# Attention output kept in weight slots and stored once per pair, with reordered start, gating and end, in a fused attention and mixture-of-experts kernel

## Chip, cores and metric

The kernel runs on one core of a Trainium2 chip. The metric is the device time of one execution in microseconds (us), lower is better. All inputs and outputs lie in HBM.

## What is computed

The reference runs three layers one after the other: attention over 4 batches, 8 heads, 576 positions and 64 dimensions, then a mixture of experts in which each token goes to one expert of at most 288 tokens, then a second mixture of experts with 32 slots.

```
attn = softmax(q_d k_d) v_d, repeated 4 times along the positions   # q_d, k_d, v_d: means over 4 positions
     + softmax over |i - j| < 4 of (q k) times v
x    = attn as 2304 rows of 512
logits = x @ w_gate                     # 8 experts
assigned = greedy by falling logit, at most 288 tokens to an expert
y[mask_e] = relu(x[mask_e] @ w1[e]) @ w2[e]
logits2 = y @ phi                       # 32 slots
d = softmax of logits2 over the tokens;  c = softmax over the slots
slot_out[e] = relu((d.T @ y)[e] @ m2w1[e]) @ m2w2[e]
out = c @ slot_out
```

## The kernel before, in words

Everything is written by hand: each stage is a function, and lists of stage names fix the order in which every engine gets its instructions. An engine runs its own instructions in that order and waits where one needs something. There are four parts.

**Attention** (`attention`, lines 37 to 376). The work is cut into 8 units; a unit is two heads by two batches, and 4 units make a pair of batches. One unit loads `k` (two transfers, 576 KB together), `q` (576 KB), `v` (1008 KB) and `vp` (two transfers, 640 KB), 2800 KB in all; SyncE (SP) issues these loads. GpSimd makes the sums over 4 positions (`pool_k`, `pool_q`, `pool_v`). TensorE makes the banded scores (`l_scores`, lines 120 to 133, which opens with the mask matmul of L126 and goes on with 72 matmuls of L131), the coarse scores (`d_scores`), transposes (`l_tr`, `d_tr`) and products with the values (`d_av`, `l_av`, line 282). VectorE takes maxima, sums and divisions (`l_max`, `d_max`, `l_norm`, `d_norm`) and adds both results to `xT` (`l_add`); ScalarE does the exponentials (`l_exp`, `d_exp`) and copies out of PSUM (`l_tr`, L216; `d_tr_out`; `d_out`). `l_x` (lines 305 to 313) transposes `xT` back in three groups of three tiles and ScalarE copies each group into the tile `xu`, of which there are two buffers: unit u writes the buffer of unit u - 2. `l_st` (lines 322 to 325) stores `xu` of a unit to `x_dram` in HBM; ScalarE issues this transfer, 576 KB in runs of 512 bytes. `l_logit` and `l_lg` make the gate logits.

The order is `FIRST` (unit 0 and the start of unit 1), then `UNIT0` once, then `UNIT` for units 1 to 8, where the second entry is relative to the period's unit. A period of `UNIT` holds `l_scores` of the next unit early and `d_tr` of the next unit late, `l_x(0, 0)` of its own unit, `l_x(-1, 1)`, `l_x(-1, 2)` and `l_st(-1)` of the unit before, the loads of the unit two ahead, and at its end `pump`, which loads one weight half (1 MB, `w2t`) into a free slot in periods 2 to 6 and fills all free slots in period 7.

**Weight slots** (`Stream`, lines 862 to 919). All expert weights are streamed in halves of 1 MB through named slots of SBUF: `a0` to `a8`, `b0` to `b7`, and tiles of the attention that have become free (`V2`, `kT1`, `V0`). `pump` pairs the next weight on the list with the next free slot and has SP issue the load; `release` gives a slot back. SP takes its transfers in program order, so one that waits holds back those behind it.

**Gating** (`gating`, lines 583 to 858). Five rounds move thresholds until each expert has at most 288 tokens; a round is a chain through VectorE, ScalarE and TensorE. TensorE fills its free time with `PMaker.product` (lines 517 to 528): 16 products `P` of `phi` and the `w2t` halves, of 32 matmuls each (L525), taken off PSUM by `turn` (L537, VectorE). Before: two products after the first transposes, two in each of the five rounds, one after the sums of `dispatch`, three at the end of `dispatch`; two `turn` in each round, two in `dispatch` ahead of L756, one ahead of L776, three at the end. `dispatch` (lines 739 to 791) computes the rows of each expert (`totals`: L698, L699), writes `idx`, and calls `first_gather`, three indirect transfers that fetch expert 0's rows of `x_dram`. Then a branch (L851) on all engines asks whether more rounds are needed.

**Experts and end** (`moe`, lines 1151 to 1487). `START`, `PERIOD`, `END` and `LAST` order the stages of the 8 experts: `x_t` (transposes of the gathered rows), `split` (weights into two parts: ScalarE L1196, VectorE L1198), `hidden` (TensorE, L1211 to L1214), and so on down to `weighted` (L1309) and `slots` (L1331). In `weighted` four PSUM tiles `m`, `l`, `g`, `t` are written (`m`, `l`, `h`, `t` for the last expert). `l` is also what `soft_lt` (L1274) reads. `FINISH` orders the second layer's own work: `c_load` loads the logits `lg`, `c_soft` is their softmax on VectorE, `first` (L1427), `first_t` (L1438), `second` (L1449), `gathered`, `combine` (L1479).

Of the kernel before, what the change touches and what calls it, by code (L numbers as in the profile page):

```python
# [36 lines left out]
def attention(nc, tc, ctx, kv, q, k, v, vp, C, x_dram, logit_tok, wg, pump):  # L37
# [296 lines left out]
    stages = dict(load_k=load_k, load_q=load_q, load_v=load_v, load_p=load_p, pool_k=pool_k, pool_q=pool_q, pool_v=pool_v,  # L334
# [23 lines left out]
    load_p(0)  # L358
    load_v(0)
# [44 lines left out]
UNIT0 = [
    ("l_tr", 0, 0),
    ("l_tr", 0, 1),
    ("load_v", 2),
    ("pool_q", 1),
    ("d_av", 0),
    ("load_p", 2),  # L410
    ("d_out", 0),
    ("l_max", 1),
    ("d_scores", 1),
    ("d_max", 1),
    ("pool_v", 1),
    ("l_exp", 1),
    ("l_norm", 1),
    ("d_exp", 1),
    ("l_tr", 0, 2),
    ("d_norm", 1),  # L420
    ("l_av", 0),
    ("pump", 0),
    ("d_tr", 1),
    ("l_add", 0),
    ("pool_q", 2),
    ("l_x", 0, 0),
]
UNIT = [
    ("d_tr_out", 0),
    ("load_k", 2),  # L430
    ("pool_k", 1, 0),
    ("pool_k", 1, 1),
    ("load_q", 2),
    ("l_scores", 1),
# [18 lines left out]
    ("load_p", 2),
    ("l_x", 0, 0),
    ("l_x", -1, 2),
    ("l_norm", 1),
    ("l_lg", -1),
# [53 lines left out]
class PMaker:  # L511
# [71 lines left out]
def gating(nc, tc, ctx, L, C, Z, idx, fill, first, force=None):  # L583
# [10 lines left out]
    def psum(shape):  # L594
        return ps.tile(shape, F32, name="t", bufs=4)
# [15 lines left out]
    fill.products(psum)  # L611
# [44 lines left out]
    def rounds(n, start=False):  # L656
        for r in range(n):
# [12 lines left out]
            fill.turn()  # L670
            fill.turn()
# [16 lines left out]
            fill.products(psum)  # L688
# [233 lines left out]
def halves(kind, es):  # L922
# [15 lines left out]
    ("first_t", 0, 1),  # L938
# [703 lines left out]
```

## Time and profile before

| what | us |
|---|---|
| median of 3 runs (424.38 to 428.44) | 428.37 |
| the profiled execution | 427.75 |
| its span, first to last instruction | 426.0 |
| mean granted TensorE clock of the span, share of full | 0.917 |
| TensorE busy | 360.7 (85%) |
| VectorE, ScalarE, GpSimd busy | 235.9, 180.5, 127.4 |

All times in the rows further down count from the span's start. The profiled execution lies 0.62 us under the median and has 1.75 us around its span. Attention reaches to 150.4, gating to 195.9, the experts to 375, the end to 426. A busy share is an average over stages with different limits, so each stage has to be read by itself: the timeline names in square brackets how long an engine was idle before an instruction and what ended that.

### The profile page before, as it was taken

The numbers are of one execution on the slowest core, as the hardware profiler recorded it, in microseconds if no ns is written. First come the engines' busy times: TensorE is split into PE (matmuls) and PEld (weight loads), VectorE is DVE, ScalarE is ACT, GpSimd is POOL, SyncE is SP. The second block draws the span as 40 slices with busy tenths as digits, with TensorE's granted clock in tenths as the row PEclk, the third lists the DMA queues.
The fourth block names the chain that finished last, engine by engine and source line by source line (L and its number), as shares of the span: only waits on it lengthen the run. The fifth ranks groups of instructions, "written<-read, shape, count | busy, mean of one in ns | idle before, by whom it ended". The sixth has DMA issues, their size and how long they took to land. (4 is left out here: it accounts for less than half of the span.)

```text
span 426.0 us, 12313 instructions
## 1 busy us (share of the span) xinstructions
PE 360.7 (85%) x5116; PEld 270.1 (63%) x5116; DVE 235.9 (55%) x636; ACT 180.5 (42%) x497; POOL 127.4 (30%) x167
## 2 busy tenths in 40 slices
PE   0779989899559876757899999999999898689994
PEld 0456666666328556656878787887879685233693
DVE  4653647645505189763456676665758475424253
ACT  6362765567135434103545454453636343101231
POOL 6466663725340000042205050505141102240000
PEclk9885999989855899966999999999999999989997
DMA  8999978798997798934485999999997696989965
GB/s 230 274 268 246 205 201 274 226 291 264 260 397 275 226 382 310 425 109 161 157 295 195 329 333 335 353 360 323 363 321 254 230 390 267 373 320 411 408 244 217
DMA packets 31962, 122.52 MB, mean 288 GB/s; under 512 B 3232, under 2 KB 13088, under 8 KB 22688
## 3 DMA queue, kind: packets, MB, share of 16 engines
q1 hardware_dynamic: 19968, 111.85, 76.7%
q10 hardware_dynamic: 9632, 4.85, 4.1%
q0 software_dynamic: 2304, 5.02, 4.0%
q8 instruction: 41, 0.67, 0.7%
q14 instruction: 17, 0.14, 0.1%
HBM read 111.97 MB, written 9.73 MB: 286 GB/s over the span
## 5 line engine op out<-in xcount | busy, mean ns | idle before, releaser
L1293 POOL DMA_INDIRECT lg_rows<-lt,idx x24 | 24.6, 1026 | 114.0 <-DVE lt L1274 109.1
L1211 PE MATMUL h<-V,wh 128*128 128x288 f32 x128 | 37.9, 317 | 2.3 <-ACT V L1188 1.1
L1211 PE MATMUL t<-V,wh 128*128 128x288 f32 x128 | 37.9, 318 | 1.6 <-ACT wh L1196 1.6
L1212 PE MATMUL h<-V,wh 128*128 128x288 f32 x128 | 36.5, 306 | 0.5 <-DVE a L887 0.5
L1212 PE MATMUL t<-V,wh 128*128 128x288 f32 x128 | 35.0, 296 | 0.0
L216 ACT ACTIVATE aT<-t 38x384 f32<-38x384 f32 (+1 forms) x48 | 21.5, 448 | 26.4 <-PE t L212 25.6
L1198 DVE TENSOR_TENSOR wl<-b,wh 128x512 fp32r<-128x512 f32 x32 | 21.7, 682 | 18.7 <-ACT wh L1196 18.5
L1211 PEld LDWEIGHTS t<-V,wh 128*128 128x128 f32 x128 | 24.1, 188 | 8.5 <-issue 5.7
L1226 DVE STREAM_TRANSPOSE V<-hT 128x288 f32<-128x288 f32 x64 | 27.1, 453 | 4.1 <-issue 4.1
L1211 PEld LDWEIGHTS h<-V,wh 128*128 128x128 f32 x128 | 25.1, 196 | 6.4 <-issue 2.8
L1198 DVE TENSOR_TENSOR wl<-a,wh 128x512 fp32r<-128x512 f32 x32 | 21.7, 678 | 11.2 <-ACT wh L1196 10.7
L180 DVE TENSOR_REDUCE lg<-D 128x6 f32<-128x864 f32 x8 | 8.5, 1067 | 34.6 <-PE D L172 34.6
L1196 ACT ACTIVATE wh<-b 128x512 fp32r<-128x512 f32 x32 | 20.0, 631 | 16.4 <-DVEq L851 10.5
L1175 POOL DMA_INDIRECT kT<-x_dram,idx x21 | 20.2, 963 | 21.0 <-PE t L1186 17.0
L1212 PEld LDWEIGHTS h<-V,wh 128*128 128x128 f32 x128 | 25.2, 197 | 0.8 <-DVE a L887 0.8
L1220 ACT ACTIVATE hT<-h 128x288 f32<-128x288 f32 x32 | 13.1, 409 | 29.7 <-PE m L1243 15.3
L1212 PEld LDWEIGHTS t<-V,wh 128*128 128x128 f32 x128 | 24.1, 189 | 0.1
L1196 ACT ACTIVATE wh<-a 128x512 fp32r<-128x512 f32 x32 | 20.3, 633 | 8.5 <-PE h L1212 5.0
L282 PE MATMUL S<-aT,V 102*64 102x64 f32 x512 | 19.4, 239 | 5.0 <-ACT aT L216 2.9
L1214 PE MATMUL h<-V,wl 128*128 128x288 f32 x128 | 22.8, 301 | 0.0
L313 ACT ACTIVATE xu<-t 128x384 f32<-128x384 f32 x24 | 10.8, 485 | 27.9 <-DMA x_dram<-xu 17.4
L282 PEld LDWEIGHTS S<-aT,V 102*64 102x64 f32 x512 | 17.9, 152 | 7.3 <-ACT aT L216 3.1
(310 smaller groups left out, 963.5 us busy)
## 6 DMA issues: line engine op xcount, KB each, us to landing
a<-in_moe_w_dram SPq DMA_DIRECT2D x27, 1024.0 KB, 7.8
b<-in_moe_w_dram SPq DMA_DIRECT2D x21, 1024.0 KB, 12.1
a<-in_moe_w2t_dram SPq DMA_DIRECT2D x9, 1024.0 KB, 8.7
V<-in_v_dram SPq DMA_DIRECT2D x8, 1008.0 KB, 12.8
kT<-in_k_dram SPq DMA_DIRECT2D x16, 288.0 KB, 11.5
qT<-in_q_dram SPq DMA_DIRECT2D x8, 576.0 KB, 12.8
x_dram<-xu ACTq DMA_DIRECT2D x8, 576.0 KB, 13.7
vp<-in_vp_dram SPq DMA_DIRECT2D x8, 512.0 KB, 13.6
```

The source lines that it names most:

```text
L216: nc.scalar.activation(aT[sl, 3 * g:3 * g + n, :, r], p[sl, 0:n].rearrange("p s (c q) -> p s c q", c=4), AF.Copy)
L282: nc.tensor.matmul(p[64 * h:64 * h + 64, k // 2, o:o + 64], rows_v(s, slice(0, 64 + W), 2 * k + h, c), aT[0:64 + W, 2 * k + h, c].rearrang ...
L313: nc.scalar.activation(s["xu"][:, 3 * g:3 * g + 3], p, AF.Copy)
L1175: nc.gpsimd.indirect_dma_start(out=xs[0:96, DM * c:DM * c + DM], out_offset=None, in_=x_dram, in_offset=bass.IndirectOffsetOnAxis(ap=idx[: ...
L1196: nc.scalar.activation(wh, w, AF.Copy)
L1198: nc.vector.tensor_sub(wl, w, wh.bitcast(F32))
L1211: nc.tensor.matmul(p, wh[:, dt], xh[:, dt], start=dt == 0, stop=False)
L1212: nc.tensor.matmul(p, wh[:, dt], xl[:, dt], start=False, stop=False)
L1214: nc.tensor.matmul(p, wl[:, dt], xh[:, dt], start=False, stop=dt == 3)
L1220: nc.scalar.activation(h, st.pop(("ph", e, ft)), AF.Relu)
L1226: nc.vector.transpose(st["hb", e][:, :, ft], st.pop(("hr", e, ft)).rearrange("p (b t) -> p b t", t=32))
L1293: nc.gpsimd.indirect_dma_start(out=lg_rows[3 * e + c], out_offset=bass.IndirectOffsetOnAxis(ap=idx[:, 3 * e + c:3 * e + c + 1], axis=0), i ...
```

## The change

Six parts. (1) `xu` is gone: the four units of a pair write their 128 columns of `x` into shared tiles of full rows, two weight slots (`a5`, `a6` for the first pair, `a7`, `a8` for the second) and a small tile `xu8`. `l_x` takes groups of 4, 4 and 1 tiles. (2) `l_st` only does something for the last unit of a pair: SP, no longer ScalarE, issues three transfers with runs of 8 KB (2 KB for the third), 2.36 MB together. The weight stream has `a0` to `a4` during attention, gets `a5`, `a6` in period 7 and `a7`, `a8` behind `b7`. In `UNIT` the `pump` comes ahead of `load_p` and `l_st` behind it. (3) `FIRST`, `UNIT0` and `UNIT` are reordered; `warm` issues matmuls whose result nobody reads, 10, 16 and 10 in `FIRST`. (4) Gating: three products at first, two in four rounds, one in the fifth, four after `totals`; rounds take all made products off, `dispatch` only at its end; five PSUM buffers in place of four. (5) `warm` in the experts' first period (8, then 2 after each of two `x_t`) and in `LAST` (2, 3, 2, 3); `weighted` of the last expert uses `m`, `h`, `h`, `t`. (6) `FINISH`: `first_t` follows its `first` closer, and `second(3, 1)` and `gathered(3, ...)` come ahead of `combine(2, ...)`.

```
     def l_x(u, g):
-        s = st[u]
-        xT = s["xT"].rearrange("d b s -> d (b s)").rearrange("d (t i) -> d t i", i=128)
-        p = tpsum([128, 3, 128])
-        for i in range(3):
-            nc.tensor.transpose(p[:, i], xT[:, 3 * g + i], ident)
-        if g == 0:
-            s["xu"] = sb.tile([128, 9, 128], F32, name="xu")
-        nc.scalar.activation(s["xu"][:, 3 * g:3 * g + 3], p, AF.Copy)
+        pr, hp = divmod(u, 4)
+        xT = st[u]["xT"].rearrange("d b s -> d (b s)").rearrange("d (t i) -> d t i", i=128)
+        n = (4, 4, 1)[g]
+        p = tpsum([128, n, 128])
+        for i in range(n):
+            nc.tensor.transpose(p[:, i], xT[:, 4 * g + i], ident)
+        if hp == 0:
+            if g < 2:
+                x = wa.tile([128, 2048], F32, name=f"a{5 + 2 * pr + g}").rearrange("p (t d) -> p t d", d=DM)
+            else:
+                x = sb.tile([128, 1, DM], F32, name="xu8")
+            st["xu", pr, g] = x
+        nc.scalar.activation(st["xu", pr, g][:, :, 128 * hp:128 * hp + 128], p, AF.Copy)
...
     def l_st(u):
         pr, hp = divmod(u, 4)
-        nc.scalar.dma_start(x_dram.rearrange("(p j) d -> p j d", j=NT)[:, 9 * pr:9 * pr + 9, 128 * hp:128 * hp + 128],
-                          st.pop(u)["xu"])
+        st.pop(u)
+        if hp == 3:
+            rows = x_dram.rearrange("(p j) d -> p j d", j=NT)
+            for g in range(3):
+                n = (4, 4, 1)[g]
+                nc.sync.dma_start(rows[:, 9 * pr + 4 * g:9 * pr + 4 * g + n], st.pop(("xu", pr, g)))
...
+    def warm(u, n):
+
+        w = ident.bitcast(BF16)
+        p = tpsum([128, 256])
+        for _ in range(n):
+            nc.tensor.matmul(p, w[:, 0:128], w[:, 0:256], start=True, stop=True)
...
-    fill.products(psum)
+    for _ in range(3):
+        fill.product(psum)
...
-            fill.turn()
-            fill.turn()
+            while fill.made:
+                fill.turn()
...
-            fill.products(psum)
+            for _ in range(1 if start and r == n - 1 else 2):
+                fill.product(psum)
...
         zs, inc = totals()
+        if what is not None:
+            for _ in range(4):
+                fill.product(psum)
...
-        if what is not None:
-            fill.turn()
-            fill.turn()
-            fill.product(psum)
-
...
             u = above()
-            fill.turn()
...
-            for _ in range(3):
-                fill.product(psum)
-            for _ in range(3):
+            while fill.made:
                 fill.turn()
...
-        names = "m", "l", "g" if e < E - 1 else "h", "t"
+        names = ("m", "l", "g", "t") if e < E - 1 else ("m", "h", "h", "t")
...
+    def warm(e, n):
+
+        w = ident.bitcast(BF16)
+        p = ps.tile([128, 2, 256], F32, name="t", bufs=3)
+        for _ in range(n):
+            nc.tensor.matmul(p, w[:, 0:128], w[:, None, :].to_broadcast([128, 2, 256]), start=True, stop=True)
...
-    WS.free = [(wa, f"a{i}") for i in range(9)]
+    WS.free = [(wa, f"a{i}") for i in range(5)]
...
-                WS.free += [(kv, x) for x in ("V2", "kT1", "V0")]
+                WS.free += [(wa, "a5"), (wa, "a6")] + [(kv, x) for x in ("V2", "kT1", "V0")]
...
         WS.add_slots(wb, [f"b{i}" for i in range(8)])
+        WS.add_slots(wa, ["a7", "a8"])
```

The new order of the first unit, and what moves in the other lists:

```
FIRST: load_k 1, load_p 0, pool_k 0, l_scores 0, pool_q 0, load_q 1, load_v 0, d_scores 0, warm 10, l_max 0,
       l_exp 0, warm 16, d_max 0, load_p 1, l_norm 0, d_exp 0, load_v 1, load_k 2, pool_k (1, 0), warm 10,
       d_norm 0, l_scores 1, d_tr 0, d_tr_out 0, pool_k (1, 1), pool_v 0, load_q 2, load_v 2, l_tr (0, 0)
UNIT0: d_av 0, d_out 0, l_max 1, load_p 2, l_tr (0, 1), pool_q 1, d_scores 1, d_max 1, l_tr (0, 2), l_exp 1,
       pool_v 1, l_norm 1, d_exp 1, pump, pool_q 2, l_av 0, d_norm 1, d_tr 1, l_add 0, l_x (0, 0)
UNIT, engine by engine: l_logit(-1) behind l_tr(0, 1); d_out(0) ahead of l_tr(0, 2); pump ahead of load_p(2);
       l_st(-1) last but d_tr(1)
LAST:  warm 2 behind soft_exp, 3 behind weighted_out, 2 behind weighted_t, 3 behind slots_acc
FINISH: first 0 0, selection, c_soft, first 0 1, first_t 0 0, first 1 0, first_t 0 1, c_parts 0, first 1 1, ...
       second 3 0, second 3 1, combine 2 1, gathered 3 0, gathered 3 1, combine 2 0, combine 3 0, combine 3 1
```

## Rows read from the trace of the kernel before

**Rows 1.** Windows: stretch, its us, busy per engine, granted clock, DMA share, GB/s

```profile
100.00:120.00 20.00, 11.75 (x222) 8.51 (x218) 8.79 (x19) 7.30 (x26) 8.81 (x9) 0.83 1.04 300
...
0.00:60.00 60.00, 42.24 (x689) 29.32 (x689) 30.67 (x69) 31.93 (x89) 37.12 (x55) 0.86 1.00 246
...
67.23:80.38 13.15, 12.35 (x240) 8.68 (x235) 8.93 (x21) 7.76 (x27) 5.25 (x7) 1.00 0.97 293
...
110.00:138.50 28.50, 19.46 (x239) 13.80 (x234) 9.03 (x19) 9.82 (x31) 9.39 (x13) 0.58 0.91 314
...
138.50:150.40 11.90, 10.73 (x138) 6.96 (x136) 2.39 (x6) 5.98 (x15) 0.00 (x0) 0.86 0.75 249
...
195.90:202.00 6.10, 5.62 (x22) 5.30 (x23) 1.73 (x5) 0.93 (x2) 1.84 (x2) 0.50 0.78 269
202.00:340.00 138.00, 135.74 (x1572) 111.19 (x1571) 87.75 (x232) 67.16 (x164) 36.16 (x36) 1.00 0.86 296
...
376.20:379.50 3.30, 3.30 (x20) 0.87 (x16) 0.00 (x0) 0.00 (x0) 2.70 (x11) 0.50 1.00 415
```

The columns after the us are busy us (and instructions) of PE, PEld, DVE, ACT and POOL; a DMA share of 1.00 is all 16 engines busy.

**Rows 2.** Waits of ACT and of SP: us in total, times, longest us

```profile
ACT xu L313 <- DMA x_dram<-xu: 17.4, 3, 11.8
...
SPq L891 <- DMA x_dram<-xu: 66.4, 6, 14.4
...
SPq L88 <- DMA x_dram<-xu: 11.6, 1, 11.6
```

**Rows 3.** DMA issues between 97 and 103: size, us from issue to landing

```profile
x_dram<-xu ACTq DMA_DIRECT2D x1, 576.0 KB, 22.1
```

**Rows 4.** Timeline of ACT and PE, units 5 to 7: start, us, engine, line

```profile
97.30 0.42 ACTq L324 DMA_DIRECT2D x_dram<-xu  x1
...
110.00 0.47 PE L126 MATMUL S<-mask,identb 128*128 128x380 bf16 x2
...
112.76 2.09 PE L131 MATMUL S<-kT,qT 128*32 128x76 f32 x72 [2.30 <-DMA qT<-in_q_dram]
...
119.47 0.87 ACT L313 ACTIVATE xu<-t 128x384 f32<-128x384 f32 x2 [11.77 <-DMA x_dram<-xu]
```

**Rows 5.** Timeline of PE, end of the first unit

```profile
32.62 1.12 PE L282 MATMUL S<-aT,V 102*64 102x64 f32 x16 [2.92 <-ACT aT L216]
...
38.16 0.78 PE L126 MATMUL S<-mask,identb 128*128 128x380 bf16 x2
```

**Rows 6.** Timeline from the last round of gating to the first expert

```profile
177.90 0.38 DVE L644 TENSOR_TENSOR Z<-key,best 128x72 bf16<-128x72 f32 x2
178.93 0.42 PE L698 MATMUL g<-Z,onesb 128*128 128x144 bf16 x1
...
180.88 0.50 DVE L537 STREAM_TRANSPOSE P<-t 128x128 f32<-128x128 f32 x2
...
189.39 0.92 POOL L1146 DMA_INDIRECT kT<-x_dram,idx  x1 [0.30 <-remote]
...
192.23 0.32 DVE L537 STREAM_TRANSPOSE P<-t 128x128 f32<-128x128 f32 x1 [1.18 <-PE t L525]
...
195.92 0.61 PE L1211 MATMUL h<-V,wh 128*128 128x288 f32 x1 [1.14 <-ACT V L1188]
```

**Rows 7.** DMA issues between 186 and 194: us from issue to landing

```profile
kT<-x_dram,idx POOLq DMA_INDIRECT x3, 3.5
```

**Rows 8.** Timeline of PE and DVE, last expert and end

```profile
366.62 0.37 PE L1309 MATMUL l<-V,dT 32*32 32x256 f32 x1 [0.94 <-DVE lt L1274]
...
381.57 0.75 DVE L1394 TENSOR_REDUCE cmx<-lg 128x18 f32<-128x576 f32 x1 [6.32 <-DMA lg<-lg_rows]
...
385.83 0.69 DVE L1169 TENSOR_SCALAR h<-h 128x512 f32<-128x512 f32 x1
...
388.57 0.62 PE L1427 MATMUL h<-kT,sT 128*32 128x512 f32 x1 [0.74 <-ACT h L1167]
...
418.43 0.63 PE L1479 MATMUL h<-R,V 128*128 128x128 f32 x4 [1.09 <-DVE R L1467]
```

More of the change, by code (lines that the diff above doesn't have):

```diff
@@ L34, in dap, with attention @@
     return bass.AP(tensor=t.tensor, offset=t.offset + offset, ap=[list(d) for d in dims])
-def attention(nc, tc, ctx, kv, q, k, v, vp, C, x_dram, logit_tok, wg, pump):
+def attention(nc, tc, ctx, kv, wa, q, k, v, vp, C, x_dram, logit_tok, wg, pump):
     ident = C["ident"]
@@ L380 @@
     ("load_k", 1),
+    ("load_p", 0),
     ("pool_k", 0, 0),
+    ("pool_k", 0, 1),
+    ("l_scores", 0),
+    ("pool_q", 0),
     ("load_q", 1),
-    ("pool_k", 0, 1),
-    ("pool_q", 0),
+    ("load_v", 0),
     ("d_scores", 0),
+    ("warm", 0, 10),
+    ("l_max", 0),
+    ("l_exp", 0),
+    ("warm", 0, 16),
     ("d_max", 0),
     ("load_p", 1),
+    ("l_norm", 0),
     ("d_exp", 0),
-    ("l_scores", 0),
     ("load_v", 1),
-    ("l_max", 0),
+    ("load_k", 2),
+    ("pool_k", 1, 0),
+    ("warm", 0, 10),
     ("d_norm", 0),
-    ("pool_k", 1, 0),
-    ("l_exp", 0),
+    ("l_scores", 1),
     ("d_tr", 0),
     ("d_tr_out", 0),
-    ("load_k", 2),
+    ("pool_k", 1, 1),
     ("pool_v", 0),
-    ("pool_k", 1, 1),
-    ("l_norm", 0),
     ("load_q", 2),
-    ("l_scores", 1),
+    ("load_v", 2),
+    ("l_tr", 0, 0),
 ]
 UNIT0 = [
[L405 to L408, printed above, removed]
     ("d_av", 0),
-    ("load_p", 2),
     ("d_out", 0),
     ("l_max", 1),
+    ("load_p", 2),
+    ("l_tr", 0, 1),
+    ("pool_q", 1),
     ("d_scores", 1),
     ("d_max", 1),
+    ("l_tr", 0, 2),
+    ("l_exp", 1),
     ("pool_v", 1),
-    ("l_exp", 1),
     ("l_norm", 1),
     ("d_exp", 1),
-    ("l_tr", 0, 2),
+    ("pump", 0),
+    ("pool_q", 2),
+    ("l_av", 0),
     ("d_norm", 1),
-    ("l_av", 0),
-    ("pump", 0),
     ("d_tr", 1),
     ("l_add", 0),
-    ("pool_q", 2),
     ("l_x", 0, 0),
@@ L437 @@
     ("l_max", 1),
-    ("load_v", 2),
+    ("load_q", 2),
+    ("l_tr", 0, 1),
     ("l_logit", -1),
-    ("l_tr", 0, 1),
     ("l_exp", 1),
     ("d_scores", 1),
+    ("d_max", 1),
+    ("d_out", 0),
     ("l_tr", 0, 2),
-    ("d_out", 0),
-    ("d_max", 1),
+    ("pool_v", 1),
+    ("l_av", 0),
     ("d_exp", 1),
-    ("l_av", 0),
+    ("load_v", 2),
+    ("l_x", -1, 1),
     ("l_add", 0),
-    ("l_x", -1, 1),
     ("d_norm", 1),
-    ("pool_v", 1),
-    ("pool_q", 2),
[L453 to L457, printed above, removed]
+    ("l_norm", 1),
+    ("l_x", 0, 0),
+    ("l_lg", -1),
+    ("l_x", -1, 2),
+    ("pump", 0),
+    ("load_p", 2),
+    ("pool_q", 2),
     ("l_st", -1),
     ("d_tr", 1),
-    ("pump", 0),
 ]
@@ L594, in psum @@
     def psum(shape):
-        return ps.tile(shape, F32, name="t", bufs=4)
+        return ps.tile(shape, F32, name="t", bufs=5)
     mm = one.tile([128, 2], F32, name="mm")
@@ L932 @@
     ("first", 0, 1),
+    ("first_t", 0, 0),
     ("first", 1, 0),
-    ("first_t", 0, 0),
+    ("first_t", 0, 1),
     ("c_parts", 0),
@@ L959 @@
     ("second", 3, 0),
+    ("second", 3, 1),
     ("combine", 2, 1),
-    ("second", 3, 1),
-    ("combine", 2, 0),
     ("gathered", 3, 0),
     ("gathered", 3, 1),
+    ("combine", 2, 0),
     ("combine", 3, 0),
@@ L1129 @@
     ("soft_exp", -1),
+    ("warm", -1, 2),
     ("soft_d", -1),
@@ L1135 @@
     ("weighted_out", -1),
+    ("warm", -1, 3),
     ("weighted_sum", -1),
     ("weighted_t", -1),
+    ("warm", -1, 2),
     ("slots", -1),
     ("slots_acc", -1),
+    ("warm", -1, 3),
 ]
@@ L1341, in slots_acc @@
             nc.vector.scalar_tensor_tensor(acc, acc, cor[e % 2], p, op0=ALU.mult, op1=ALU.add)
-    def psum(shape):
-        return ps.tile(shape, F32, name="t", bufs=3)
-    stages = dict(hidden=hidden, relu=relu, split=split, x_t=x_t, gather=gather, h_rows=h_rows,
+    def warm(e, n):
[3 more added lines that the diff above has]
+            nc.tensor.matmul(p, w[:, 0:128], w[:, None, :].to_broadcast([128, 2, 256]), start=True, stop=True)
+    stages = dict(warm=warm, hidden=hidden, relu=relu, split=split, x_t=x_t, gather=gather, h_rows=h_rows,
                   logits2=logits2, logits2_out=logits2_out, soft=soft, soft_exp=soft_exp, soft_d=soft_d, soft_lt=soft_lt, scatter=scatter, weighted=weighted, weighted_out=weighted_out, weighted_sum=weighted_sum,
@@ L1360, in moe @@
             split(0, 2)
+            warm(e, 8)
         for name, rel, *args in START if e <= 0 else PERIOD if e < E - 1 else END if e < E else LAST:
@@ L1363, in moe @@
                 stages[name](e + rel, *args)
+                if e == -1 and name == "x_t" and args[0] < 2:
+                    warm(e, 2)
                 if (name, e + rel) == ("weighted_out", E - 1):
@@ L1543, in pump @@
                 WS.once += ["V2", "V0"]
-                WS.free += [(kv, x) for x in ("V2", "kT1", "V0")]
+                WS.free += [(wa, "a5"), (wa, "a6")] + [(kv, x) for x in ("V2", "kT1", "V0")]
             WS.pump((0, 0, 1, 1, 1, 1, 1, None)[u])
-        attention(nc, tc, actx, kv, q, k, v, vp, C, x_dram, L, wg, pump)
+        attention(nc, tc, actx, kv, wa, q, k, v, vp, C, x_dram, L, wg, pump)
     wb = ctx.enter_context(tc.tile_pool(name="wb", bufs=1, reuse_waits="tile"))
```

15 lines of the change are left out of this document (4 added, 11 removed).

## Prediction

> **What bounds the kernel now.** I read the windows first, then the waits, the DMA issues of the place where they are long, and the timelines around it. The windows [rows 1] show two kinds of stretch. From 202 to 340 TensorE is busy 135.74 of 138 us at the full clock: it is the bound there, the change touches nothing in it, and it can only be shifted as a block. Before 150.4 it is otherwise: an undisturbed attention period (67.23 to 80.38) takes 13.15 us with 12.35 of PE, but the last full one (110 to 138.5) takes 28.50 with 19.46 of PE at a granted clock of 0.58. Something starves it, and the clock falls with it.
>
> The waits say what [rows 2]: ScalarE's copy into `xu` waits 17.4 us in three pieces, the longest 11.8, for the store of `x`, and SP's loads wait 66.4 and 11.6 us for the same stores, since they get their completion behind them. The DMA view gives the cause [rows 3]: a 576 KB store takes 22.1 us to land. The timeline puts it together [rows 4]: the store issued at 97.30 lands near 119.4, and the copy at 119.47 has stood 11.77 us for it. With it stands all that ScalarE issues behind (exponentials, copies of transposes), and so PE. Before that, the scores of unit 7 opened at 110.00, but their matmuls waited 2.30 us for `q` and came at 112.76: DMA was at a share of 1.04 [rows 1]. So two bounds lie close together up to 110: PE's period and the load stream. Which of them is late once the stall goes is the main question.
>
> **Attention, part by part.** The profiled execution took 427.75 us, 0.62 under the median; I sum against it and add 0.62 at the end.
>
> (a) First unit. `l_av` (L282) waits 2.92 us for ScalarE's copies, which stand behind `l_exp(1)` [rows 5]; the new order has `l_tr(0, 1)` ahead of them and `l_tr(0, 2)` ahead of `l_exp(1)`. That gives 2.9, and a further 1 us from the clock, which is 0.86 over 0 to 60 [rows 1]: unit 2's mask matmul comes at 34 in place of 38.16 (-4). The 36 `warm` matmuls lie in gaps of PE (42.24 busy of 60 [rows 1]). No row has this form; by the 0.78 us of a pair of L126 [rows 5] (380 columns, against 256) one takes 0.13 to 0.26, all 36 between 4.7 and 9.5 us. If the cover is gone, (a) is worth +1 to +5; if the clock comes up at once, -7.
>
> (b) The stall. No store comes before the last unit of a pair, and no tile is written twice in a pair, so the 17.4 us of ScalarE's waits go, and SP's waits on stores too. From 38.16 to 110.00 are five periods of 14.4 us; at 13.15 each, PE would open unit 7 at 34 + 65.8 = 99.8.
>
> (c) What is late next: `q` of unit 7. Ahead of its landing lie seven units (7 x 2.867 MB), `k` and `q` (1.18), three weight halves (3.15) and the first pair's store (2.36): 26.8 MB. Two rows bound the rate. At 246 GB/s all along (0 to 60, share 1.00) it lands at 108.8; with 60 us at 246 (14.8 MB) and the other 12.0 MB at 300 (100 to 120) at 100.0. Both rows are saturated with the same kinds of load, so neither is nearer: 104.4, the middle, against 112.76 before.
>
> (d) From there to the end. L126 would stand at 103.9 as if unhindered; plus 13.15, plus the last part: 11.90 us at clock 0.86 [rows 1], so about 28% of its 10.73 us of PE ran at half clock, 1.4 less without: 10.5. That is 127.6. But PE has waited some 4 us for `q`, and such idling before had the clock at half; a half-clock stretch like 195.9 to 202 is 6.10 us long [rows 1], and costs half of that: +3. End at 130.6 against 150.4: **-19.8**. Bounds: nothing late and full clock, 99.8 + 13.15 + 10.5 = 123.5 (-26.9); `q` at 108.8, and PE work stretched as in 110 to 138.5 (19.46 against 12.35, +7.1) with the last part as before, 108.3 + 13.15 + 7.1 + 11.9 = 140.5 (-9.9).
>
> (e) Costed at nothing. `l_x` in 4, 4 and 1 tiles has the same nine transposes, and three copies of other sizes; the copies of 3 tiles have 0.87 for two [rows 4], so a third more for two and a third for one: the same sum, and ScalarE has slack (7.76 of 13.15 busy [rows 1]). The pair's store is three DMAs on SP, and waits there for ScalarE's last copy; behind it stand `k` and `q` of unit 7 (first pair), `b0` to `b7` (second). It comes behind `load_p`, and the copy it needs is issued ahead of `pump`, so it should find it done; if not, each us of it is one of (c). The rest of `UNIT` leaves each engine's order nearly as it was; the loads move inside one period, under 13 us of a two-period lead.
>
> **Gating.** The order of the products moves one behind `totals`: PE's L698 came at 178.93, 0.65 after Z ended (178.28), behind the product of 177.79 [rows 6] (-0.65). The `turn` inside the chain (0.50 at 180.88) goes to the end (-0.5). So the gathers come 1.1 earlier; the third was issued at 189.39, with 3.5 us to landing [rows 7], thus 191.8. Before, the last `turn` waited 1.18 us for a product, ended at 192.55, and all engines took the branch behind it; hidden opened at 195.92. Now the four products lie in front, beside VectorE's chain, and the branch no longer waits; what ends last is the third gather, plus its transposes and the copy that PE waited 1.14 us for: 193.0. **-2.9** (bounds -1.1, if the branch isn't sooner, and +3, if four products of 1.2 us push PE's part of `dispatch` back).
>
> The loads behind it: six `w2t` halves are now in `b0` to `b5`, behind the second store. 8.65 MB at 300 to 415 GB/s [rows 1] are 21 to 29 us after the end E of attention; the last product needs its half near E + 31 (`totals` at E + 28, three products). Hidden, by a small margin.
>
> **Experts' start.** 195.9 to 202 runs at clock 0.50 with 5.62 busy [rows 1]; full clock gives up to 2.8. The 8 + 4 warm matmuls lie while PE waits for the gathers. **-1.7** (0 to -2.8, +1 if they stand ahead of the transposes).
>
> **Last expert and end.** `weighted` no longer waits for `lt` (0.94 at 366.62 [rows 8]) and the 3.30 us at half clock (376.2 to 379.5 [rows 1]) may go up to 1.65 down; the 0.74 before L1427 at 388.57 goes with the move of `first_t`. But VectorE stands 6.32 us for `lg` until 381.57 in `c_soft`, and its evacuation for the next `first` comes at 385.83 + 0.69 = 386.5, whatever PE does before: the matmul at 388.57 can gain 2.0 at most. At the very end the 1.09 us before L1479 (418.43) is filled by moved work: -1.2. **-3.2** (0 to -4.4).
>
> **Sum.** 19.8 + 2.9 + 1.7 + 3.2 = 27.6; 427.75 - 27.6 + 0.62 = 400.8, **forecast 401**, its own range 397 to 405.
>
> **The rivals.**
> DMA-bound (411): the store was not the cause, only what was seen to be late in a full stream; 26.8 MB come at 246, (d) at its upper bound: -9.9 - 2.9 - 1.7 - 3.2 = -17.7. For it: share 1.00 to 1.04 in 0 to 60 and 100 to 120, 22.1 us for 576 KB, and `x` keeps its bytes. Against it: SP stood 78 us for stores, in which it put nothing more into the stream, and 67.23 to 80.38 moves 293 GB/s. [...]
>
> The clock isn't kept (405): `warm` is in the trace of nothing before, and if its short matmuls don't raise the granted clock, experts' start (1.7) and the 1.65 of the end stay and (a) loses 1: 401 + 4.
>
> All holds (392): attention -26.9, gating -2.9, start -2.8, end -4.4: -37 to 391.4.
>
> Nothing changes (427): the loads that SP then issues sooner fill the same 16 engines and unit 7 stays at 112.76, the last part at half clock.
>
> Slower (435): SP's head of line. The stores now stand in the queue of all loads and wait there for ScalarE. If the first one stands a period (13.15) before `k` and `q` of unit 7, these land at 117.5, and with the low clock (+7.1, last part 11.9) attention ends at 149.2 (-1.2); behind the second, with one more half still on its way at E, 9.70 MB at 246 GB/s put `b5` at E + 39, 8 us after `dispatch` wants it, and gating, the experts' clock and the end give nothing: 427.75 - 1.2 + 8 + 0.62 = 435. It decides from `q` after 117 and `b5` after E + 31. For it: SP's program order and a DMA share near 1. Against it: the copies stand a period ahead.
>
> **How the numbers follow.** Forecast 0.45; DMA-bound 0.22; clock not kept 0.12; all holds 0.12; nothing changes 0.05; slower 0.04. The range, 391 to 414, takes in the first four with the bounds of gating and start. A measurement of this kernel can tell about 1% (4.3 us) from no change: faster by more 0.91, within 0.05, slower by more 0.04.
>
> **What would show it.** Right: ScalarE waits for no `x_dram`, the scores of unit 7 (L131 before) near 104, attention's end at 131, periods of 13.2 us; the sums of `dispatch` (L698 before) 20 to 21 us earlier; clock over 0.7 in the first 6 us of the experts; 138 us of experts unchanged; no gap ahead of the last `combine`. Wrong: `q` of unit 7 after 108 or a clock of 0.58 behind it; SP waiting for ScalarE's copies; a product in gating that waits for a `b` half; `warm` with a gap of PE behind it and the clock still at half.

## The result, and the profile after

The changed kernel takes 409.12 us (median of 4 runs, 404.65 to 412.61), the kernel before 428.4 beside it: ratio 0.949, 95% interval 0.938 to 0.961. It is faster, inside the range (391 to 414), 8 us over the forecast of 401. Executions of one kernel come in a faster and a slower state (here 404.65 and 407.34 against 410.89 and 412.61), and ratios with their intervals compare the faster ones alone, so they differ from the quotient of the medians; every trace shown of the whole kernel is of a faster run, but for that of experiment 11. The profiled execution of after took 407.34 us, span 405.6.

The windows cut both kernels at the same events: unit 2's and unit 7's mask matmul, end of attention, first hidden matmul, the sums (L1320 before, L1336 after) of the last expert but one and of the last, the end. Columns as in [rows 1]. Before:

```profile
0.00:38.20 38.20, 21.72 (x333) 15.68 (x334) 19.75 (x47) 19.25 (x49) 23.95 (x41) 0.82 0.98 256
38.20:110.00 71.80, 65.30 (x1172) 45.42 (x1170) 41.51 (x89) 42.76 (x144) 36.84 (x43) 0.95 0.89 245
110.00:150.30 40.30, 30.16 (x375) 20.76 (x370) 11.38 (x24) 15.70 (x46) 9.39 (x13) 0.66 0.86 294
150.30:195.90 45.60, 29.31 (x669) 24.98 (x668) 34.81 (x140) 12.19 (x38) 7.29 (x8) 0.92 0.74 277
195.90:355.00 159.10, 154.72 (x1770) 128.10 (x1770) 98.46 (x263) 74.31 (x182) 40.75 (x41) 0.98 0.87 304
355.00:369.40 14.40, 11.29 (x162) 6.24 (x162) 8.93 (x30) 4.56 (x13) 2.05 (x3) 1.00 0.77 294
369.40:426.00 56.60, 48.21 (x644) 28.91 (x644) 21.11 (x48) 11.76 (x27) 7.13 (x20) 0.92 0.82 320
```

After:

```profile
0.00:36.80 36.80, 25.23 (x369) 19.25 (x370) 19.67 (x47) 19.07 (x49) 20.34 (x37) 0.90 0.97 233
36.80:111.60 74.80, 66.76 (x1172) 48.93 (x1169) 41.23 (x89) 43.69 (x146) 40.49 (x47) 0.91 1.03 262
111.60:138.60 27.00, 23.16 (x375) 15.74 (x369) 11.43 (x24) 14.31 (x44) 9.42 (x13) 0.94 0.86 306
138.60:182.20 43.60, 32.17 (x680) 25.36 (x680) 35.27 (x141) 12.62 (x38) 6.70 (x9) 0.92 0.91 356
182.20:338.60 156.40, 152.25 (x1773) 125.78 (x1773) 98.00 (x261) 74.35 (x182) 39.98 (x41) 1.00 0.88 310
338.60:351.10 12.50, 11.82 (x167) 6.34 (x167) 8.42 (x29) 4.34 (x13) 0.80 (x1) 1.00 0.69 258
351.10:405.60 54.50, 47.83 (x650) 28.56 (x649) 21.38 (x49) 11.92 (x28) 8.38 (x22) 0.96 0.87 347
```

| stretch | forecast | measured |
|---|---|---|
| attention | -19.8 | -11.7 |
| gating to first hidden | -2.9 | -2.0 |
| experts' start | -1.7 | -2.7 |
| last expert and end | -3.2 | -4.0 |
| sum | -27.6 | -20.4 |

All of the miss is in attention, and there ahead of unit 7: its mask matmul comes at 111.62, where (c) had 103.9. The first unit gave 1.4 us in place of 4, and from unit 2 to unit 7 it now takes 74.80 us, 3 more than before, where (b) had 65.8. After unit 7 the forecast's number holds: 27.00 us in place of 40.30.

The stall of [rows 2, 4] is gone: ScalarE waits nowhere for `x_dram`. In its place SP stands for ScalarE's copies before a pair's store (the view of waits, us in total, times, longest). Ahead of the first store, between 87.9 and 96.8, it stands 6.7 us for `a` and 0.6 for `xu`; the 12.6 lies ahead of the second, until 137.4:

```profile
SPq L334 <- ACT xu L318: 14.7, 3, 12.6
...
SPq L334 <- ACT a L318: 6.7, 1, 6.7
```

The rows that answer to [rows 4] and [rows 6], TensorE's and GpSimd's timeline of after (start, us, engine, line):

```profile
111.62 0.47 PE L126 MATMUL S<-mask,identb 128*128 128x380 bf16 x2
113.01 1.34 PE L131 MATMUL S<-kT,qT 128*32 128x76 f32 x67 [0.92 <-DMA qT<-in_q_dram]
...
166.72 0.42 PE L715 MATMUL g<-Z,onesb 128*128 128x144 bf16 x1
...
177.23 1.05 POOL L1162 DMA_INDIRECT kT<-x_dram,idx  x1 [0.31 <-issue]
...
182.24 0.40 PE L1227 MATMUL h<-V,wh 128*128 128x288 f32 x1 [0.58 <-ACT V L1204]
```

`q` of unit 7 comes as late as before (113.01 against 112.76), but PE stands only 0.92 us for it: the unit itself opens no sooner than 111.62. So two questions were open: why the load stream is no faster with the stall gone, and what makes the five periods 14.96 us each on average (74.8 / 5).

### The profile page after: what moved, and what is told of

Read it like the earlier page. It is cut to its first block, busy times and chain, and to the rows that moved or that the text cites. A ratio compares the mean times of both kernels' runs of the same rounds, so it can differ in the third digit from the quotient of the medians.

```text
span 405.6 us, 12412 instructions
## 1 busy us (share of the span) xinstructions
PE 359.2 (89%) x5174; PEld 270.0 (67%) x5174; DVE 235.4 (58%) x636; ACT 180.3 (44%) x497; POOL 126.1 (31%) x167
## 5 line engine op out<-in xcount | busy, mean ns | idle before, releaser
L1227 PE MATMUL h<-V,wh 128*128 128x288 f32 x128 | 36.4, 306 | 1.7 <-ACT wh L1212 1.1
L1228 PE MATMUL h<-V,wh 128*128 128x288 f32 x128 | 35.0, 296 | 0.2 <-DVE a L899 0.2
L1214 DVE TENSOR_TENSOR wl<-a,wh 128x512 fp32r<-128x512 f32 x36 | 24.5, 681 | 15.5 <-ACT wh L1212 15.1
L1227 PEld LDWEIGHTS h<-V,wh 128*128 128x128 f32 x128 | 24.0, 188 | 5.9 <-issue 2.8
L1212 ACT ACTIVATE wh<-a 128x512 fp32r<-128x512 f32 x36 | 22.8, 633 | 10.7 <-PE h L1228 7.6
L1191 POOL DMA_INDIRECT kT<-x_dram,idx x21 | 19.8, 943 | 17.0 <-PE t L1202 11.1
L1236 ACT ACTIVATE hT<-h 128x288 f32<-128x288 f32 x32 | 13.1, 409 | 26.9 <-PE m L1259 15.3
L1228 PEld LDWEIGHTS h<-V,wh 128*128 128x128 f32 x128 | 24.1, 188 | 0.4 <-DVE a L899 0.4
L114 POOL TENSOR_TENSOR halfv<-vp 128x768 f32<-128x768 f32 x8 | 14.5, 1815 | 27.0 <-DMA vp<-in_vp_dram 24.3
L299 DVE TENSOR_TENSOR xT<-S,up 128x512 f32<-128x512 f32 x16 | 10.3, 685 | 21.6 <-PE S L282 21.6
L1214 DVE TENSOR_TENSOR wl<-b,wh 128x512 fp32r<-128x512 f32 x24 | 16.1, 679 | 11.1 <-ACT wh L1212 9.9
L1230 PE MATMUL t<-V,wl 128*128 128x288 f32 x128 | 22.3, 295 | 0.0
## 6 DMA issues: line engine op xcount, KB each, us to landing
b<-in_moe_w_dram SPq DMA_DIRECT2D x21, 1024.0 KB, 12.2
V<-in_v_dram SPq DMA_DIRECT2D x8, 1008.0 KB, 18.1
vp<-in_vp_dram SPq DMA_DIRECT2D x8, 512.0 KB, 18.1
```

The costliest lines, as they stand in the source:

```text
L1191: nc.gpsimd.indirect_dma_start(out=xs[0:96, DM * c:DM * c + DM], out_offset=None, in_=x_dram, in_offset=bass.IndirectOffsetOnAxis(ap=idx[: ...
L1212: nc.scalar.activation(wh, w, AF.Copy)
L1214: nc.vector.tensor_sub(wl, w, wh.bitcast(F32))
L1227: nc.tensor.matmul(p, wh[:, dt], xh[:, dt], start=dt == 0, stop=False)
L1228: nc.tensor.matmul(p, wh[:, dt], xl[:, dt], start=False, stop=False)
L1230: nc.tensor.matmul(p, wl[:, dt], xh[:, dt], start=False, stop=dt == 3)
```

## The experiments

**1 and 2. The stores by themselves, and all but the stores.** The first is the kernel before with the new `l_x`, `l_st` and slot lists; the second the changed kernel with the old ones.

> The kernel before with parts 1 and 2 alone (x kept in weight slots, one store per pair by SP). Theory 'stream': the stores are the whole gain of attention; what is late behind them is q of unit 7 in the load stream, so q lands near 113 us as in both kernels, attention ends at 138 to 141 in place of 150.3, and the time falls by 9 to 12 us (ratio 0.972 to 0.979). Rival 'order': the new order of FIRST and UNIT and the warm matmuls carry part of it; then attention ends after 143 here and the ratio is above 0.983.

> The changed kernel with the stores of before (one of 512-byte runs per unit, issued by ScalarE, xu in two buffers). Theory 'stream': ScalarE waits for x_dram again, over 10 us in all, and attention ends within 3 us of 150.3; the rest of the change still gives 8 to 9 us (gating 2, start of the experts 3, end 4), ratio 0.978 to 0.984. Rival 'order': attention ends before 146 although the stores are as before, ratio below 0.975.

The stores alone: 419.04 us against 426.88 (medians); ratio 0.977, from too few runs for an interval, where the theory had 0.972 to 0.979. Windows:

```profile
0.00:37.80 37.80, 21.00 (x334) 15.02 (x335) 19.75 (x47) 19.27 (x49) 24.04 (x41) 0.95 0.98 253
37.80:109.90 72.10, 64.38 (x1171) 45.35 (x1170) 41.47 (x89) 43.42 (x146) 37.00 (x44) 0.98 0.98 253
109.90:138.10 28.20, 24.45 (x374) 16.49 (x369) 11.38 (x24) 14.28 (x44) 9.14 (x13) 0.88 0.83 304
```

Attention ends at 138.1: the stores alone reach the whole gain there (-12.2), and with them the new order with its `warm` adds none. All but the stores: 417.56, ratio 0.979 (0.971 to 0.987). There the stall is back, in the waits and the timeline of ScalarE:

```profile
ACT xu L313 <- DMA x_dram<-xu: 20.8, 3, 15.0
...
119.16 0.87 ACT L313 ACTIVATE xu<-t 128x384 f32<-128x384 f32 x2 [15.03 <-DMA x_dram<-xu]
```

Its attention ended at 145.8, 4.5 us sooner than before. That is beyond the 3 us of the theory and inside the bound of the rival 'order' (146), though the ratio isn't under its 0.975: without the new stores the order does give something, so the two gains don't add up. Everything up to the stall was early: unit 7 opened at 106.43, 5 us ahead of the changed kernel, with the old stores. That pointed at the stream.

**3. The loads by themselves.** No computation: units' loads back to back on SP, with other work beside them by stretch.

> Not the computation: only the loads of attention, 5 units in a row in each of five stretches (14.3 MB each), then 12 weight halves; the output holds what the stores of these stretches leave. Stretch 1: loads alone. 2: with a store of 512-byte runs per unit on ScalarE's queue. 3: GpSimd busy with sums of the size of pool_q and pool_v. 4: VectorE, ScalarE and TensorE busy. 5: all four. In the changed kernel's attention these loads move at about 230 GB/s with the DMA engines full. Theory 'shape': the loads' own shape sets it, 220 to 250 GB/s in stretch 1 too. Rival 'contention': 300 GB/s or more in stretch 1, and 220 to 250 only where engines are busy, by GpSimd alone (3) or by the others (4). Side question: if a store beside the loads costs its own share of the engines, stretch 2 is longer than 1 by 2.9 MB at the stretch's rate (about 10 us); if it slips in beside them, by under 4 us.

Windows inside the stretches 1, 2 (while stores run, then behind them), 3, 4, 5 and the weight halves:

```profile
5.00:65.00 60.00, 0.00 (x0) 0.00 (x0) 3.03 (x5) 0.00 (x0) 0.00 (x0) 1.00 0.96 228
66.00:88.00 22.00, 0.00 (x0) 0.00 (x0) 0.00 (x0) 1.28 (x1) 0.00 (x0) 1.00 1.06 319
88.00:123.00 35.00, 0.00 (x0) 0.00 (x0) 0.00 (x0) 0.00 (x0) 0.00 (x0) 1.00 1.01 293
125.00:192.00 67.00, 0.00 (x0) 0.00 (x0) 0.00 (x0) 0.00 (x0) 56.35 (x40) 1.00 0.97 214
194.00:255.00 61.00, 61.00 (x532) 61.00 (x531) 58.14 (x85) 58.02 (x93) 0.00 (x0) 1.00 0.99 236
261.00:321.00 60.00, 60.00 (x540) 60.00 (x539) 58.94 (x32) 57.08 (x91) 60.00 (x33) 1.00 0.99 240
376.00:403.00 27.00, 0.00 (x0) 0.00 (x0) 0.00 (x0) 0.00 (x0) 0.00 (x0) 0.50 1.01 421
```

'Shape' holds here: with the compute engines nearly idle, the loads fill the DMA engines (share 0.96) at 228 GB/s; busy engines leave that about as it is (214 to 240). Weight halves take the same engines at 421. The side question came out beyond what I had asked: with short stores on the other queue the total rises to 319, and the loads stay at 293 when the stores have ended.

**4. Fewer bytes ahead of `q`.**

```diff
-            WS.pump((0, 0, 1, 1, 1, 1, 1, None)[u])
+            WS.pump((0, 0, 0, 0, 0, 1, 2, None)[u])
```

> The changed kernel, but the weight halves of periods 2 to 4 (3 of 1 MB, all ahead of q of unit 7) are loaded in periods 6 and 7 in place of them. Theory 'stream': q of unit 7 lands 8 to 10 us earlier (103 to 105 in place of 112.9), attention ends 7 to 10 us earlier (129 to 132), and the time falls by as much unless gating then waits for a late half: ratio to before 0.925 to 0.935. Rival 'periods': attention is bound by its engines' own order, the halves are hidden, attention ends within 2 us of 138.6, ratio 0.945 to 0.955. Rival 'head of line': what holds q is SP's wait for ScalarE's copies at the pair's store (8.6 us, from 87.9 to 96.8); then q moves by under 3 us.

406.32 us, ratio 0.949 (0.942 to 0.955): as the changed kernel. `q` landed at 107.0, 5.9 us sooner than in the changed kernel's trace, unit 7 opened at 111.39 all the same, and attention ended at 136.8, within 2 us of 138.6. So the rival 'periods' holds, and an early `q` of unit 7 is worth next to nothing. The late halves aren't shown to be what brought `q` forward: in experiments 7 and 8, which load them where the changed kernel does, it landed at 108.0 and 107.2, and unit 7 opened at 111.2 and 111.4. The windows of its last two periods before unit 7, and `l_av` of the first of them:

```profile
85.20:98.30 13.10, 12.22 (x242) 8.79 (x235) 7.54 (x17) 8.52 (x29) 8.24 (x8) 1.00 0.62 211
98.30:111.40 13.10, 12.21 (x241) 8.79 (x236) 8.91 (x20) 8.52 (x29) 4.00 (x5) 1.00 1.01 285
...
91.97 2.09 PE L282 MATMUL S<-aT,V 102*64 102x64 f32 x64 [0.40 <-ACT sc L151]
```

These two are undisturbed: 13.1 us at full clock. The other three took 14.5, 16.7 and 17.6. In the changed kernel the same `l_av` is cut in two.

**What cuts it: a place in TensorE's code.** The gaps over 0.3 us of the changed kernel's TensorE between 50 and 100 that no visible event ends:

```profile
59.09 0.32 PE L212 MATMUL t<-ident,sc 128*102 128x128 f32 x1 [1.85 <-issue]
...
75.92 1.62 PE L282 MATMUL S<-aT,V 102*64 102x64 f32 x47 [0.74 <-issue]
...
83.25 0.95 PE L131 MATMUL S<-kT,qT 128*32 128x76 f32 x42 [0.40 <-issue]
...
92.41 1.04 PE L282 MATMUL S<-aT,V 102*64 102x64 f32 x29 [2.02 <-issue]
```

Ahead of them lie 1473, 1985, 2241 and 2497 of TensorE's records (matmuls, weight loads and its sequencer's own): 512, 256 and 256 apart. If they belong to a place in the code, taking 36 `warm` matmuls out ahead must move them by 36 matmuls. Experiment 7 does that:

```profile
76.70 0.56 PE L282 MATMUL S<-aT,V 102*64 102x64 f32 x11 [1.19 <-issue]
...
85.48 0.33 PE L131 MATMUL S<-kT,qT 128*32 128x76 f32 x6 [2.27 <-issue]
```

The gap after 17 of 64 matmuls is now after 53 of 64, the one after 30 of 72 after 66 of 72: both by 36, and at the same counts of records, 1985 and 2241. The trace also has the packets of a DMA queue that the page of the changed kernel lists as `instruction` (packets, MB):

```profile
q8 instruction: 42, 0.69, 0.7%
```

They are 16 KB each, and every one of the four gaps ends 1.4 to 1.5 us after one of them has landed:

| records ahead | packet landed | TensorE goes on | gap |
|---|---|---|---|
| 1473 | 57.72 | 59.08 | 1.85 |
| 1985 | 74.41 | 75.92 | 0.74 |
| 2241 | 81.81 | 83.25 | 0.40 |
| 2497 | 90.91 | 92.41 | 2.02 |

So at these four records TensorE goes on only when a packet has landed. That the packets hold its code is my reading of the queue's name, of the counts and of the shift in experiment 7; no run shows what is in them. The length of a gap is a matter of when the packet comes: in experiment 4 the one for record 2497 landed at 91.32, 1.69 us ahead of TensorE, and there was no gap; in the changed kernel the packets for records 961, 1217 and 1729 landed 2.5 to 2.8 us ahead, without a gap over 0.3 us too. Call TensorE's step into the next 256 records a crossing: in the changed kernel, between units 2 and 7, the next packet starts 4.4 to 6.3 us after a crossing, with the DMA share at 1.02 to 1.03; in experiment 4, where the DMA engines stood idle at the crossing behind record 2497, it started after 0.9 us, and in the kernel before, at record 1473 (62.01), after 1.35 us with the share at 0.17. Of the nine crossings of the changed kernel between units 2 and 7, TensorE stood over 0.3 us at four. A full stream doesn't bring a gap each time: the second of the undisturbed periods of experiment 4 had a share of 1.01.

Behind the two long gaps TensorE's granted clock was 0.50: from 59.79 to 66.62, and from 93.93 to 97.34. The windows of the changed kernel's periods of units 3, 4 and 5, with gaps of 1.85, 0.74 and (0.40, 2.02):

```profile
51.00:67.70 16.70, 14.85 (x241) 11.44 (x234) 9.02 (x19) 8.85 (x29) 11.80 (x20) 0.80 1.03 249
67.70:81.70 14.00, 12.45 (x240) 8.91 (x234) 8.04 (x20) 8.61 (x29) 7.83 (x8) 1.00 1.03 255
81.70:98.10 16.40, 13.58 (x240) 9.99 (x234) 8.63 (x19) 8.71 (x29) 6.80 (x7) 0.90 1.03 262
```

The four gaps sum to 5.0 us. PE's busy time over the five periods is 66.76, against 61.1 at full clock (5 x 12.22): 5.7 more. Together 10.7, which is enough for the 9.3 us by which 74.8 exceeds five periods of 13.1. Of the 5.7, 1.1 lie in the first of the five periods (13.32 us busy, clock 0.91), ahead of these gaps.

**5. What a short store does to the loads.**

> Not the computation: again 5 units of attention's loads per stretch, no engine busy; the output holds what the stores leave. 1: SP alone (control). 2: q and vp issued by ScalarE, k and v by SP. 3: a store of 2 MB in 8 KB runs on ScalarE's queue beside every second unit. 4: one store of 512-byte runs (576 KB) at the start, then loads alone. 5: a store of 512-byte runs per unit on SP's own queue. The run before showed 223 GB/s alone and 293 GB/s still 35 us after short-run stores on ScalarE's queue had ended. Theory 'in step': the 16 DMA engines working through one queue in step get in each other's way, and anything that takes them out of step helps: 4 and 5 over 270 GB/s, 2 over 260. Rival 'second queue': it needs a second queue with work: 2 and 3 over 260, 5 like the control (220 to 240), and 4 falls back after the store. Rival 'chance': the stretch was fast for another reason; 2 to 5 all at 215 to 245.

The barrier held only SP's loads, and the loads and stores that ScalarE issued ran ahead into the stretch before, so 1 and 2 are mixed and settle nothing on the second queue. The stores of 3 were issued from 81 to 108, and from 118 its loads ran alone behind them. The windows of this, of 4 (behind its one store) and of 5:

```profile
118.00:168.00 50.00, 0.00 (x0) 0.00 (x0) 1.00 1.03 293
...
177.00:221.00 44.00, 0.00 (x0) 0.00 (x0) 1.00 1.03 297
225.00:286.00 61.00, 0.00 (x0) 0.00 (x0) 1.00 1.04 270
```

(The busy columns are VectorE and GpSimd here.) Behind the one store of 512-byte runs on ScalarE's queue the loads ran at 297 GB/s for the rest of the stretch, but they had run at 293 before it, behind stores of 8 KB runs: this one store isn't shown to have done anything, and short runs aren't shown to be needed. The same short stores on SP's own queue give 270 with the stores counted in, about 224 for the loads alone (14.3 of 17.3 MB). 'In step' expected 4 and not 5 to come out so, 'second queue' 5 and not 4: neither is shown, and what a store changes between the engines stays open.

**6. Three buffers for the old stores.** The changed kernel with the old `l_x` and `l_st`, `bufs=3` for `xu`, and `b8` for `a8`.

> The changed kernel with the stores of before (per unit, 512-byte runs, ScalarE's queue) but three buffers xu in place of two (the slot a8 becomes b8 to make room). Theory 'short stores help the loads': ScalarE has no wait for x_dram worth naming, q of unit 7 lands near 106 as in the run with two buffers, the scores of unit 7 open near 106.5 and attention ends at 130 to 133 against 138.6; time 6 to 8 us under the changed kernel, ratio to before 0.928 to 0.942. Rival 'SP waits': SP's loads and the weight halves wait for the stores' completions as before; q after 110, attention's end after 137, ratio 0.95 or above.

407.01 us, ratio 0.957 (0.949 to 0.965). Half of the theory: attention ended at 134.6, 4 us sooner, and the gaps were fewer, but SP still stood 60 us for the stores, as the rival said, and unit 7 waited for `q`:

```profile
107.95 2.51 PE L131 MATMUL S<-kT,qT 128*32 128x76 f32 x72 [2.40 <-DMA qT<-in_q_dram]
```

The 4 us were not to be seen in the time. They are little more than one trace can tell: experiment 8 has the attention of the changed kernel unaltered, and there it ended at 135.6.

**7 and 8. The clock, the end, gating.** The first takes out every `warm` and puts the old `FINISH` back; the second puts back gating and the tile names of the last `weighted`.

> The changed kernel without any warm matmul, and with the order FINISH of before. Read by stage. If warm keeps the clock up: from the first hidden matmul to the last pw sums of the experts 171 to 172 us in place of 168.9 (before: 173.5), and first unit as slow as or slower than before. If it does nothing: 169. FINISH: from VectorE's wait for lg to the end 44 to 45 us in place of 41.4 (before 44.5). In sum 4 to 6 us over the changed kernel, ratio 0.960 to 0.966; if neither does anything, 0.949.

> The changed kernel with the gating of before (products, turns, four PSUM buffers) and the tile names m, l, h, t in the last weighted. Theory: gating from the end of attention to the first hidden matmul 45.5 us in place of 43.7, the last expert about 1 us longer; 2 to 4 us in all, ratio 0.953 to 0.960. Rival: attention now ends sooner while the weight halves come no sooner, so that the old order, which wants its last products later, loses nothing: under 1 us.

Without `warm`: 410.34, ratio 0.966 (0.959 to 0.973). From first hidden to the last sums 170.6 us against 168.9: `warm` at the start of the experts is worth 1.7 by these two traces, and the granted clock shows it (without, then with):

```profile
182.00:202.00 20.00, 18.08 (x117) 16.28 (x118) 7.96 (x20) 8.28 (x18) 4.58 (x5) 0.89 0.68 233
```

```profile
182.20:202.00 19.80, 17.68 (x128) 15.97 (x129) 9.18 (x22) 8.58 (x19) 4.16 (x5) 1.00 0.78 249
```

In the first unit it isn't shown to be worth anything: attention ends at 137.2 without it. From the last sums to the end it is 55.7 against 54.5, so `warm` in `LAST` and the new `FINISH` together give 1.2. From VectorE's wait for `lg` to the end it is 40.5 with the old `FINISH` against 41.4, so nothing is left for the new order by that measure.

With the old gating: 413.24, ratio 0.973 (0.965 to 0.980), slower than expected (0.953 to 0.960). Gating took 49.5 us, 6 more than in the changed kernel and 4 more than expected. As attention ended 2.9 sooner than in the changed kernel's trace, the first hidden matmul came 2.9 later (185.09 against 182.24). In experiment 1, with the same old gating and attention's end at 138.1, the stretch took 45.9, 2.3 more than in the changed kernel. Of its last three products' stretch:

```profile
171.00:180.50 9.50, 6.99 (x116) 5.96 (x116) 3.73 (x18) 0.00 (x0) 2.99 (x3) 0.54 0.33 105
```

The three products and their turns end at 179.5, at a clock of 0.54, with the gathers nearly there, and the branch stands behind them; the `warm` of the experts then comes on top instead of lying in a wait. The names `m`, `h`, `h`, `t` are worth 1.9: the last expert takes 14.42 us here, 12.56 with them.

**9 to 11. On another chip.** This chip ran the kernel before in 456.55 us (the changed kernel's experts take 180 us on it in place of 156), so only ratios are compared. Experiment 9 adds one short store ahead of `FIRST`, 10 joins 4 and 6, 11 is the changed kernel again.

```diff
+    nc.scalar.dma_start(x_dram.rearrange("(p j) d -> p j d", j=NT)[:, 0:9, 0:128], z.rearrange("p (j d) -> p j d", d=128))
     for name, u, *args in FIRST:
```

> The changed kernel with one store of 576 KB in 512-byte runs (zeros, into rows of x_dram that the first pair's store writes over later) issued by ScalarE at about 11 us, ahead of the first unit's exponentials. In the loads alone such a store at the start left the stream at 296 GB/s for 50 us, against 215 without. Theory 'in step' carried over: the stretch from 20 to 60 rises from 230 to 280 GB/s or more, q of unit 7 lands before 102, TensorE's code gaps shrink and attention ends at 129 to 133: ratio 0.925 to 0.94. Rival: SP's pauses and the other queues undo it within one or two units; 225 to 250 GB/s from 40 on, attention's end 134 to 139, ratio as the changed kernel's, 2 us of DMA more.

> Both together: per-unit short stores by ScalarE with three xu, and the weight halves of periods 2 to 4 loaded in periods 6 and 7. With three xu alone unit 7 waited 2.4 us for q. Theory: that wait goes, q of unit 7 lands near 101, attention ends at 131 to 133 in place of 134.6; ratio 0.94 to 0.953. Rival: gating then waits for late halves or the experts for theirs, the gain is given back, ratio 0.955 to 0.965.

> The changed kernel once more, on the chip of the two others, to set them against. Theory 'code': TensorE's gaps that nothing visible ends come at the same instructions as in the first profile (3rd transpose of l_tr near 59, after 17 of 64 matmuls of l_av near 76, after 35 of 64 near 92), with other lengths, and attention ends at 135 to 139.

The changed kernel: ratio 0.966 (0.947 to 0.984). With the start store 0.974 (0.965 to 0.983), and no faster stream, as the rival had it (window of 40 to 60):

```profile
40.00:60.00 20.00, 16.90 (x289) 11.67 (x287) 10.60 (x22) 12.26 (x38) 12.37 (x12) 0.97 1.03 232
```

So what went with faster loads in experiments 3 and 5 doesn't carry over. Three buffers with late halves: 0.986 (0.977 to 0.995), the highest of the three, though the intervals overlap. A store landed after 28.3 us, and ScalarE stood at the issue of the next one (73.63) until then:

```profile
74.06 0.60 ACT L247 ACTIVATE eT<-D 112x512 f32<-112x512 f32 x1 [11.88 <-DMA x_dram<-xu]
```

So a third buffer takes away the wait for the tile, and not the one at the issue. In the trace of the kernel before, SP's issues show such a wait too: the weight half issued at 64.00 waits for the semaphore of the store that landed at 63.99, and carries it itself. The gaps of the changed kernel came back on this chip at the same matmuls, with other lengths, and attention ended at 141.2, later than expected:

```profile
58.12 0.37 PE L212 MATMUL t<-ident,sc 128*102 128x128 f32 x1 [2.77 <-issue]
...
74.97 2.56 PE L282 MATMUL S<-aT,V 102*64 102x64 f32 x47 [1.36 <-issue]
...
92.34 1.76 PE L282 MATMUL S<-aT,V 102*64 102x64 f32 x29 [1.58 <-issue]
```

No version tried is shown to beat the changed kernel.

## Why the prediction was right, and where it was not

**(b), the stall: right in the mechanism, wrong in the size.** ScalarE's wait is gone, and experiment 1 reaches the whole gain of attention with the stores alone. The step that failed is the five periods "at 13.15 each": they took 14.96 on average. The 13.15 was one undisturbed period out of a trace whose stream was often idle (DMA share 0.89 between units 2 and 7, now 1.03). With the stall gone SP keeps the stream full, the packets that TensorE stands for start 4.4 to 6.3 us behind a crossing, and behind each of the two long gaps the clock was 0.50, for 6.8 and 3.4 us.

**(c), `q` of unit 7: wrong too.** The forecast counted from `q` at 104.4; it came at 112.9, outside both bounds (100.0 and 108.8). The 300 GB/s of the better bound was read from a stretch with short stores in it; those were what the change took away, and the loads alone ran at 228. TensorE's periods and `q` were about equally late (111.62 and 112.9), so either would have cost most of the miss; with `q` at 107.0 to 108.0 (experiments 4, 7 and 8) unit 7 opened no sooner than 111.2. Of the signs of being wrong that the prediction named, this one came, and SP's wait for ScalarE's copies. Why the loads are no faster stays open.

**(d), unit 7 to the end: right in the number**, 27.0 us against 26.7 (from 103.9 to 130.6), and partly by luck: its 3 us were for a wait of some 4 us for `q`, which took 0.92.

**(a), first unit: too large** in this trace, -1.4 in place of -4; the clock between 20 and 40 stayed low (0.74), and the 36 `warm` aren't shown to bring anything there. In experiment 8 the same order opened unit 2 at 33.29, 3.5 sooner than in the changed kernel's trace, and lost it again by unit 4 (67.22 against 67.73), behind a longer gap at the same record, 1473:

```profile
57.60 0.45 PE L212 MATMUL t<-ident,sc 128*102 128x128 f32 x1 [3.32 <-issue]
```

**Gating** gave 2.0 of 2.9. The sums came 0.4 sooner behind attention (forecast 0.65). The turn inside the chain gave nothing: the third gather is issued 10.5 us behind the sums, as before. The branch gave the rest. With attention as short as it is now, the old gating took 2.3 more in experiment 1 and 6 more in experiment 8, where it met a clock of 0.54; so what the part is worth depends on when attention ends.

**Experts' start** gave 2.7 against 1.7 (`warm` 1.7 of it), **last expert and end** 4.0 against 3.2, of which 1.9 are the names.

**The rivals.** DMA-bound named 411, and the time is nearer to it than to the forecast; its stream was as full and `q` as late as it said, but experiment 4 shows that an early `q` isn't enough: behind the full stream come TensorE's gaps as well, 5.0 us in four. What the queue of a store is worth to the rate stays open: with short stores beside the loads on ScalarE's queue the DMA engines moved 319 GB/s in all (experiment 3), with stores of the same form on SP's own queue 270 (experiment 5). 'Slower' saw its head of line: ahead of the first store SP stood 6.7 us for copies, but a load lay 18.1 us (median of `v`) between issue and landing, and the stream never ran dry there (share 1.03 from 81.7 to 98.1). The 12.6 us ahead of the second store came when no load of attention was left. The stream did run low in experiment 4, with less in hand (share 0.62).

## What to carry to other kernels

A transfer that an engine must wait for, behind a deep queue, is worth taking off its path even at the same bytes: that was 12 us here. But one undisturbed period, from a trace whose DMA is often idle, isn't the period that you get when the change fills the DMA: look which of TensorE's gaps end in "issue", count the records between them (256 and 512 here), and price them with the clock behind them (here 0.50 for 6.8 and 3.4 us behind the two long ones, 1.00 behind the two short ones). And a rate read from a mixed stretch belongs to the mixture: 300 GB/s there, 228 for the loads alone.

## What was not expected of the hardware

Alone on SP's queue, the loads of attention filled the DMA engines at 214 to 240 GB/s whether the compute engines worked or not (experiment 3), and at 293 to 297 for 35 us and more after stores on ScalarE's queue (experiments 3 and 5); in the kernel itself one such store at the start did nothing (232 GB/s, and 230 without it in experiment 11). The packets of the queue `instruction` are 16 KB each, and TensorE's gaps that end in "issue" lay 256 and 512 of its records apart; behind a full load stream such a gap took up to 3.3 us (experiment 8), and in each of the four gaps of the changed kernel TensorE went on 1.4 to 1.5 us after a packet had landed.
